# An attention, expert layer and MLP kernel: a new start, new numbers for the order of attention, weight subtracts on one engine, a second bank for transposes of x, and a shifted second tile in the last chunk

## The chip, the cores and the metric

The kernel runs on one core of one Trainium2 chip. The time is the device time of one execution in microseconds (us): 1006.02 us before the change, the median of three runs from 1003.82 to 1007.94 us. The engines are called PE (TensorE: matmuls and transposes; its weight loads are listed apart as PEld), DVE (VectorE), ACT (ScalarE), POOL (GpSimd) and SP (SyncE, which only issues transfers here). Each has its own list of instructions and works through it in order.

## What is computed

```python
def _attn_ref(q, k, v, tau):            # q, k, v: 4 x 8 heads x 576 x 64, float32
    scores = scale * np.matmul(q, k.transpose(0, 1, 3, 2))
    thresh = np.max(scores, axis=-1, keepdims=True) - tau
    scores = np.where(scores >= thresh, scores, -1000000000.0)
    ...                                 # softmax over what is left
    return np.matmul(attn, v)

def _moe_ref(x, w_gate, w_output_gate, w1, w2):     # 2304 tokens, 512 wide, 8 experts of 1024
    e_idx = np.argmax(x @ w_gate, axis=1)           # each token goes to one expert
    ...
        h = np.maximum(x[mask] @ w1[e], 0.0)
        out[mask] = gate_w[mask, None] * eom[mask, e, None] * (h @ w2[e])

def _moe2_ref(x, w_in, w_out):                      # 2304 tokens, 512 -> 2048 -> 512
    h = x @ w_in
    return np.maximum(0.01 * h, h) @ w_out
```

The three run one after the other on the same tokens.

## The kernel before

Every fp32 factor of a product is split into two parts that PE multiplies at full rate: `hi`, a rounded copy, and `lo`, the difference between the number and its `hi` part. A product of two such factors takes three matmuls (hi by hi, hi by lo, lo by hi). So each operand costs a copy (`hi`) and a subtract (`lo`) on the engines beside PE.

The order on every engine is set ahead of time by a list planner, `Plan.run`. Each piece of work is added with the engine or engines it may run on, a cost for each, a priority (`prio`), an earliest time (`at`), the pieces it depends on, and the ring slots it takes and gives back (`Ring(n)`: n buffers or PSUM banks in turn). The planner takes, on the engine that can start soonest, the piece with the lowest priority number, and where two engines are named it takes the one that ends sooner. Its times are its own; on the chip only the order of each engine is left, and the waits on data.

There are four parts.

**Attention, 16 pairs of heads.** For a pair, k, q and v are loaded (`load`, `load_v`, tiles rk, rq, rv, by SP), split into tiles srk and srq (L310 to L317: `hi` is a CAST, `lo` a TENSOR_TENSOR; on POOL, but on ACT and DVE for pair 0), transposed on PE (L341, L367), copied out of PSUM (L250 on ACT, L252 on DVE, and L256 or L258 with the scale for q), multiplied to scores (L465), reduced to the row maximum (L474 DVE), passed through exp (L485 ACT), masked (L493 DVE), transposed (L522), and multiplied with v (L601). tile sw holds k's parts the other way round. The numbers `st.w_...` at the end of the kernel are terms of the priorities of these pieces. In the first microseconds DVE also fills some constant tiles for the router (`consts`, L770 to L787).

**The router and the seam.** The scores of the gates are made beside the last pairs, tokens are counted per expert, and the fullest expert's first 216 tokens are begun before a branch (`tc.If`) on the counts.

**The experts, in windows of 400 to 216 tokens.** SP loads weights into four `raw` tiles of 128 x 1024 in turn; `hi` (L1554, ACT or DVE) and `lo` (L1559, DVE or POOL) put them into the tile named arena. POOL gathers the tokens of a window into tiles sm (L1627). PE transposes each gathered tile of up to 108 tokens into one PSUM bank (`xt`, L1636, ring `r_tp`), from where an L1554 copy and an L1559 subtract take the parts of x out. The first layer is L1667, its relu L1675 (ACT) and L1681 (DVE), the second layer L1708. Beside this the weights of the MLP are packed into integers by L1304, L1310, L1316, L1322 (ACT) and L1326, in tiles dw and cv.

**The second MLP, chunks of 512 tokens and a last one of 256.** For each of 16 slices f of the hidden layer: the first product (L1870, `h2`), 0.01 h on ACT (L1877, `t`), the maximum on DVE (L1881, `g`), `hi` and `lo` of g (L1554, L1559), and the second product (L1896, `out`), for all token tiles of the chunk, the first product running eight slices ahead. At a chunk's end each token tile of 128 is scaled out of PSUM (L1919, `oev`) and stored to its rows by POOL (L1925, `st`). The last chunk has two token tiles, and both are finished by the last slice's six matmuls.

Of the kernel before, what the change touches and what calls it, by code (L numbers as in the profile page):

```python
# [206 lines left out]
def attention(ctx, tc, q, k, v, st):  # L207
# [61 lines left out]
    pl.add("dve", 2.0, lambda o: st.consts(o), [cnt], 10, label="consts", at=8.0)  # L269

    for P in range(NP):
# [6 lines left out]
        def load(o, P=P, b=b, h0=h0, src=None, nm=None):  # L278
            t = raw_p.tile([128, 9, D], F32, tag=nm, name=nm)
            nc.sync.dma_start(  # L280
# [3 lines left out]
            for h in range(2):  # L284
                nc.sync.dma_start(out=t[64 * h:64 * h + 64, 8, :], in_=src[b, h0 + h, 512:576, :])
# [40 lines left out]
        for nm in ("rk", "rq"):  # L326
# [1202 lines left out]
def experts(pl, ctx, tc, st, R, ar, w1, w2, w_in, w_out, xrows, yT, wtab, wf, out):  # L1529
# [8 lines left out]
    r_l1, r_tp, r_l2 = Ring(3), Ring(1), Ring(1)  # L1538
# [7 lines left out]
    def ev(n, ptr=0.0):  # L1546
        return (0.16 + 0.00083 * n + ptr, 0.14 + 0.00106 * n + ptr)
# [26 lines left out]
    for r, n, tw in wins:  # L1574
# [7 lines left out]
        for q in range(4 if r is None else 0, 8):  # L1582
# [13 lines left out]
            if r is None and q < 6:  # L1596
# [14 lines left out]
                *((("dve", "pool"), (1.5, 2.7)) if r is not None else ("dve", 1.4)), lambda o, f=lo, ld=ld, h=a: f(o, ld, h), [a], need - 11.9, rel=[(r_raw, ld)], label="lo", at=free + 3 if r is None else free)  # L1611
# [214 lines left out]
    r_o, r_g, r_t, r_h2 = Ring(1), Ring(2), Ring(2), Ring(4)  # L1826
# [5 lines left out]
    for ci, (c0, n) in enumerate(chunks):  # L1832
# [25 lines left out]
        outs = None  # L1858
        for f in range(FF // 128):
# [23 lines left out]
            def g_hi(o, tt, n=n):  # L1883
                copy(o, ar.g(o.slots[r_g][0])[:, 0, 0:n], tgs[tt.slots[r_t][0]][:, 1, 0:n])

            def g_lo(o, tt, gh, n=n):
                t = ar.g(gh.slots[r_g][0])
                subtract(o, t[:, 1, 0:n], tgs[tt.slots[r_t][0]][:, 1, 0:n], t[:, 0, 0:n].bitcast(F32))

            def prod(o, first, gh, f=f, u=u, c2=c2, m=m):  # L1890
# [15 lines left out]
            gh = pl.add(AD, (0.62, 0.4), lambda o, tt=tt, f=g_hi: f(o, tt), [gg], bf + 3.2, acq=[(r_g, 1)], label="gh")  # L1906
            gl = pl.add("dve", 0.74, lambda o, tt=tt, gh=gh, f=g_lo: f(o, tt, gh), [gh], bf + 3.3, rel=[(r_t, tt)], label="gl")
# [156 lines left out]
```

## Time and profile before

| | us |
|---|---|
| median of three runs | 1006.02 (1003.82 to 1007.94) |
| the profiled execution | 1004.9 |
| its span | 1002.7 |
| PE busy | 960.8 (96%) |
| DVE busy | 641.3 (64%) |
| ACT busy | 507.3 (51%) |
| POOL busy | 264.4 (26%) |

The profile is one execution, taken by the hardware profiler. Times in it count from the start of its span. A row of the timeline has the start and the length of a group of equal instructions on one engine, the source line, what is written and read with the shapes, the count, and in brackets the idle time ahead of it and what ended that. Line numbers are those of the kernel before. In the changed kernel the lines of attention stand one further down; of the later ones L1554 is L1555, L1559 is L1560, L1627 is L1628, L1636 is L1637, L1667 is L1668, L1708 is L1709, L1870 is L1873, L1896 is L1905.

### The profile page before, as it was taken

What the parts mean: (1) busy time and instruction counts of PE and PEld (TensorE: products, weight loads), DVE (VectorE), ACT (ScalarE), POOL (GpSimd) and SP (SyncE); (2) the same over time, 40 slices, a digit from 0 to 9 for tenths busy, and PEclk for the clock granted to TensorE, in tenths of its full rate; (3) what the DMA queues carried; (4) which work ended last, traced back from release to release, by engine and by line L of the source; (5) the groups of instructions that cost most, each with busy time, mean ns of one, the idle gap of its engine ahead of it and who ended that gap; (6) DMA issues with size and microseconds to landing.
All of it is one profiled execution on the core that took longest, in us unless ns stands there. A gap on an engine that the chain in (4) does not pass through costs nothing. (4 is left out here: it accounts for less than half of the span.)

```text
span 1002.7 us, 16909 instructions
## 1 busy us (share of the span) xinstructions
PE 960.8 (96%) x6118; PEld 844.5 (84%) x6118; DVE 641.3 (64%) x1231; ACT 507.3 (51%) x1009; POOL 264.4 (26%) x325
## 2 busy tenths in 40 slices
PE   6999999999999889999899999999999999999994
PEld 6788888888887789989899998888888888888883
DVE  7888998998996775988986548983223223222331
ACT  7778787888874355454555435443223222322321
POOL 4433333333112444442446402321000100100000
PEclk9999999999999899999999999999999999999998
DMA  5523432431242688589887552422000200100000
GB/s 143 150 71 90 129 72 74 138 81 49 75 152 69 191 222 293 190 303 305 301 286 266 166 178 77 119 70 74 11 1 1 84 1 0 63 1 1 18 25 22
DMA packets 63578, 114.32 MB, mean 114 GB/s; under 512 B 15424, under 2 KB 32832, under 8 KB 62976
## 3 DMA queue, kind: packets, MB, share of 16 engines
q1 hardware_dynamic: 56912, 92.02, 29.4%
q0 software_dynamic: 6576, 21.15, 7.6%
q8 instruction: 50, 0.82, 0.3%
q14 instruction: 40, 0.33, 0.1%
HBM read 84.72 MB, written 19.09 MB: 104 GB/s over the span
## 5 line engine op out<-in xcount | busy, mean ns | idle before, releaser
L1870 PE MATMUL ps<-arena 128*128 128x512 f32 (+1 forms) x960 | 207.6, 368 | 0.0
L1896 PE MATMUL ps<-arena 128*128 128x512 f32 x864 | 206.8, 389 | 0.0
L1870 PEld LDWEIGHTS ps<-arena 128*128 128x128 f32 x960 | 168.7, 188 | 30.9
L1559 DVE TENSOR_TENSOR arena<-raw,arena 128x512 fp32r<-128x512 f32 (+2 forms) x131 | 122.7, 941 | 111.1 <-PE ps L1896 67.0
L1896 PEld LDWEIGHTS ps<-arena 128*128 128x128 f32 x864 | 161.3, 188 | 33.2 <-ACT arena L1554 0.2
L1554 ACT CAST arena<-raw 128x1024 fp32r<-128x1024 f32 (+2 forms) x153 | 121.4, 803 | 107.5 <-PE ps L1896 56.4
L1881 DVE TENSOR_TENSOR raw<-ps,raw 128x512 f32<-128x512 f32 (+1 forms) x80 | 50.6, 636 | 134.3 <-ACT raw L1877 134.2
L1708 PE MATMUL ps<-arena 128*128 128x216 f32 (+7 forms) x864 | 128.9, 307 | 6.4 <-ACT arena L1675 4.7
L1708 PEld LDWEIGHTS ps<-arena 128*128 128x128 f32 x864 | 122.7, 193 | 7.4 <-ACT arena L1675 5.1
L1667 PE MATMUL ps<-arena 128*128 128x400 f32 (+7 forms) x768 | 114.1, 308 | 8.7 <-ACT arena L1554 3.2
L493 DVE SCALAR_TENSOR_TENSOR em<-ps,th,e 128x576 f32<-128x576 f32 x144 | 115.6, 811 | 9.2 <-ACT e L485 8.4
L1877 ACT ACTIVATE raw<-ps 128x512 f32<-128x512 f32 (+1 forms) x80 | 43.9, 553 | 150.9 <-PE ps L1870 150.9
L1667 PEld LDWEIGHTS ps<-arena 128*128 128x128 f32 x768 | 110.9, 190 | 10.3 <-DVE arena L1559 3.7
L474 DVE TENSOR_REDUCE nm<-ps 128x1 f32<-128x576 f32 x144 | 107.3, 752 | 17.0 <-PE ps L465 15.2
L485 ACT ACTIVATE e<-ps,nm 128x576 f32<-128x576 f32 x144 | 105.9, 744 | 6.8 <-DVE nm L474 6.2
L465 PE MATMUL ps<-k,qt 128*128 128x288 f32 x512 | 99.5, 322 | 2.3 <-ACT qt L256 0.9
L1925 POOL DMA_INDIRECT out_dram<-sm,oidx x18 | 17.8, 987 | 302.7 <-ACT sm L1919 269.8
L250 ACT COPY eta<-ps 128x512 f32<-128x512 f32 (+1 forms) x152 | 79.4, 543 | 23.3 <-PE ps L522 19.9
L522 PE MATMUL ps<-ident,em 128*128 128x128 f32 x576 | 84.2, 274 | 2.1 <-DVE em L493 1.3
L465 PEld LDWEIGHTS ps<-k,qt 128*128 128x128 f32 x512 | 74.6, 193 | 8.2 <-DVE em L493 2.5
L1559 POOL TENSOR_TENSOR arena<-raw,arena 128x1024 fp32r<-128x1024 f32 x23 | 58.8, 2562 | 61.7 <-ACT arena L1554 59.9
L601 PE MATMUL ps<-eta,rv 128*64 128x288 f32 x512 | 69.5, 412 | 1.9 <-ACT eta L250 1.9
(221 smaller groups left out, 1087.7 us busy)
## 6 DMA issues: line engine op xcount, KB each, us to landing
raw<-in_moe_w_dram SPq DMA_DIRECT2D x70, 512.0 KB
k<-k POOLq DMA_DIRECT2D x30, 304.0 KB
dw<-in_moe_w_in_dram SPq DMA_DIRECT2D x16, 512.0 KB
dw<-in_moe_w_out_dram SPq DMA_DIRECT2D x16, 512.0 KB
rk<-in_k_dram SPq DMA_DIRECT2D x16, 256.0 KB
rq<-in_q_dram SPq DMA_DIRECT2D x16, 256.0 KB
rv<-in_v_dram SPq DMA_DIRECT2D x16, 256.0 KB
xrows<-xt SPq DMA_DIRECT2D x4, 1024.0 KB
```

The source lines that it names most:

```text
L250: nc.scalar.copy(out=out, in_=in_)
L465: nc.tensor.matmul(out=s[:, c, :], lhsT=lhs, rhs=T[kk, P][:, off + c * HALF:off + (c + 1) * HALF], start=(m == 0), stop=(m == 2 * len(ops) ...
L474: nc.vector.tensor_reduce(out=T["nm", n], in_=T["sc", n], axis=AX.XY, op=ALU.max, negate=True)
L485: nc.scalar.activation(out=T["e", n].rearrange("p (a c) -> p a c", a=2), in_=T["sc", n], func=AF.Exp, bias=T["nm", n][:, 0:1], scale=1.0,)
L493: nc.vector.scalar_tensor_tensor(out=T["em", P, t][:, h, :].rearrange("p (a c) -> p a c", a=2), in0=T["sc", n], scalar=T["th", n][:, 0:1], ...
L522: nc.tensor.transpose(out=bank(o)[:, c * 128:(c + 1) * 128], in_=T["em", P, t][:, h, 64 * h + c * 128:64 * h + (c + 1) * 128], identity=ident,
L1554: nc.scalar.copy(out=out, in_=in_)
L1559: (nc.vector if o.eng == "dve" else nc.gpsimd).tensor_tensor(out=out, in0=in0, in1=in1, op=ALU.subtract)
L1667: nc.tensor.matmul(out=bank(o)[:, 0:n], lhsT=w[:, wi, 128 * f:128 * f + 128], rhs=xx[:, xi, c, :], start=(c == 0 and i == 0), stop=(c == K ...
L1708: nc.tensor.matmul(out=bank(first, d)[:, 0:n], lhsT=w[:, wi, k0:k0 + 128], rhs=hx[:, xi, :], start=(f == 0 and i == 0), stop=(f == 7 and i ...
L1870: nc.tensor.matmul(out=bank(o)[:, 0:n], lhsT=w[:, wi, c, 128 * c2:128 * c2 + 128], rhs=y[:, c, 0:n], start=(k == 0), stop=(k == 3 * KD - 1),)
L1896: nc.tensor.matmul(out=bank(first, t), lhsT=g[:, gi, 128 * t:128 * t + 128], rhs=w[:, wi, c2, :], start=(f == 0 and k == 0), stop=(f == FF ...
```

## The change

Five things are changed together.

- Pair 0's q is loaded on ACT's queue and no longer behind k on SP's; q's `lo` of pair 0 goes to POOL; the constants of the router may come at 1.9 and no longer at 8.0 in the planner's time.
- The numbers `st.w_...` that set the order of attention are new.
- `lo` of the experts' weights is on DVE alone, at a planned cost of 1.25 and no longer 1.5 (or 2.7 on POOL).
- The ring `r_tp` for the transposed x has two PSUM banks and no longer one.
- In the last chunk g takes half a slot (ring `r_gs`, four halves), the second product is a piece for each token tile, and the priority of the second tile's pieces lies three slices (`BEHIND`) later. The `oev` of a tile depends on that tile's last product.

```diff
-    pl.add("dve", 2.0, lambda o: st.consts(o), [cnt], 10, label="consts", at=8.0)
+    pl.add("dve", 2.0, lambda o: st.consts(o), [cnt], 10, label="consts", at=1.9)
...
-            nc.sync.dma_start(
+            eng = nc.scalar if (nm, P) == ("rq", 0) else nc.sync
+            eng.dma_start(
...
-                "sp", 1.75, lambda o, f=load, src=src, nm=nm: f(o, src=src, nm=nm),
-                [], base - 27, after=[O.get(("rk", P))],
+                "act" if (nm, P) == ("rq", 0) else "sp", 1.75, lambda o, f=load, src=src, nm=nm: f(o, src=src, nm=nm),
+                [], base - 27, after=[O.get(("rk", P)) if P else None],
...
-                *(("dve", 0.65) if P == 0 else ("pool", 1.36)), lambda o, f=lo, nm=nm: f(o, nm=nm), [a], base - 13.9,
+                *(("dve", 0.65) if P == 0 and nm == "rk" else ("pool", 1.36)), lambda o, f=lo, nm=nm: f(o, nm=nm), [a], base - 13.9,
...
-    r_l1, r_tp, r_l2 = Ring(3), Ring(1), Ring(1)
+    r_l1, r_tp, r_l2 = Ring(3), Ring(2), Ring(1)
...
-                *((("dve", "pool"), (1.5, 2.7)) if r is not None else ("dve", 1.4)), lambda o, f=lo, ld=ld, h=a: f(o, ld, h), [a], need - 11.9, rel=[(r_raw, ld)], label="lo", at=free + 3 if r is None else free)
+                "dve", 1.25 if r is not None else 1.4, lambda o, f=lo, ld=ld, h=a: f(o, ld, h), [a], need - 11.9, rel=[(r_raw, ld)], label="lo", at=free + 3 if r is None else free)
...
+            def g_at(o, n=n):
+                if n > 256:
+                    return ar.g(o.slots[r_g][0])[:, :, 0:n]
+                i = o.slots[r_gs][0]
+                return ar.g(i // 2)[:, :, 256 * (i % 2):256 * (i % 2) + n]
...
+            if small:
+                for t in range(2):
+                    o = pl.add(
+                        "pe", 3 * 0.228, lambda o, gh=gh, f=prod, fb=outs, t=t: f(o, fb or o, gh, ts=(t,)), [gl, *wo, tiles[t], outs],
+                        bf + 5.4 + 5.4 * BEHIND * t, acq=[(bk, 2), (r_o, 1)] if outs is None else [], rel=[(r_gs, gh)] if t else [], label="out")
+                    outs = outs or o
+                    tiles[t] = last_o = o
+                continue
...
-    st.w_k = [-17.57, -56.75, -17.26, -9.64, -5.15]
+    st.w_k = [-12.16, -50.35, -23.14, -10.04, -5.04]
...
```

On DVE the program begins, after some fills of tiles, with pair 0's k and q. Before the change these rows stand there (srk and srq are the split k and q, sw is k's parts swapped, qsc and ntau are made from tau):

```order
L312 CAST srk<-rk 128x9x64
L317 TENSOR_TENSOR srk<-rk,srk 128x9x64
L324 CAST sw<-srk 128x9x64
L252 CAST k_233<-ps 128x512
L317 TENSOR_TENSOR srq<-rq,srq 128x9x64
L1984 TENSOR_SCALAR qsc<-tt 128x1
L1985 TENSOR_SCALAR ntau<-tt 128x1
L770 MEMSET ones 128x128
```

After the change the same place on DVE, from the last of the constants on, reads:

```order
L785 TENSOR_SCALAR scr<-tid 128x20
L786 CAST tt<-scr 128x20
L788 MEMSET capr 128x1 x8
L313 CAST srk<-rk 128x9x64
L313 CAST srq<-rq 128x9x64
L318 TENSOR_TENSOR srk<-rk,srk 128x9x64
L2003 TENSOR_SCALAR qsc<-tt 128x1
L2004 TENSOR_SCALAR ntau<-tt 128x1
L325 CAST sw<-srk 128x9x64
L252 CAST k_273<-ps 128x512
```

All thirteen rows of constants (L771 to L788) have moved ahead of k's copy, the copy of q (before on ACT) has moved between k's copy and k's subtract, and q's subtract has gone to POOL.

On PE the first windows of the experts follow the seam. Before, the transposes of x (L1636, ident is the unit matrix, sm the gathered tokens) and the layers stand in this order, up to the first layer of the window of 400 tokens:

```order
L1708 MATMUL ps<-arena 128x216 x12
L1636 MATMUL ps<-ident,sm_70 128x108 x4
L1708 MATMUL ps<-arena 128x216 x36
L1636 MATMUL ps<-ident,sm_71 128x108 x4
L1708 MATMUL ps<-arena 128x216 x36
L1636 MATMUL ps<-ident,sm_72 128x108 x4
L1708 MATMUL ps<-arena 128x216 x12
L1636 MATMUL ps<-ident,sm_73 128x76 x4
L1667 MATMUL ps<-arena 128x400 x96
```

After the change the same place on PE reads:

```order
L1709 MATMUL ps<-arena 128x216 x12
L1637 MATMUL ps<-ident,sm_70 128x108 x4
L1709 MATMUL ps<-arena 128x216 x12
L1637 MATMUL ps<-ident,sm_71 128x108 x4
L1709 MATMUL ps<-arena 128x216 x24
L1637 MATMUL ps<-ident,sm_72 128x108 x4
L1637 MATMUL ps<-ident,sm_73 128x76 x4
L1709 MATMUL ps<-arena 128x216 x48
L1637 MATMUL ps<-ident,sm_70 128x108 x4
L1637 MATMUL ps<-ident,sm_71 128x108 x4
L1668 MATMUL ps<-arena 128x400 x96
```

The last transposes of this window's x (76 tokens of sm_73) have moved from directly ahead of its first layer to 48 matmuls ahead of it, and the first two tiles of the window after it stand there now.

On PE the program ends with the last chunk of the MLP, first products (128x256) between second products (128x512). Before:

```order
L1870 MATMUL ps<-arena 128x256 x12
L1896 MATMUL ps<-arena 128x512 x6
L1870 MATMUL ps<-arena 128x256 x12
L1896 MATMUL ps<-arena 128x512 x18
L2059 UNCONDITIONAL_BRANCH
```

After:

```order
L1873 MATMUL ps<-arena 128x256 x12
L1905 MATMUL ps<-arena 128x512 x6
L1873 MATMUL ps<-arena 128x256 x12
L1905 MATMUL ps<-arena 128x512 x27
L2078 UNCONDITIONAL_BRANCH
```

Nine more second products stand behind the last first product. By the banks they write, the last nine are the second token tile's alone (its last three slices of three matmuls), so the first tile's last product stands ahead of nine others and no longer in the last six.

On POOL the gathers of x after the seam stand one behind the other, and no weight subtracts of 128 x 1024 but one are left there; 22 have gone to DVE (23 to 1 on POOL, 51 to 73 on DVE).

## Rows read from the trace of the kernel before

**Rows 1.** Busy time by stretch: PE, PEld, DVE, ACT, POOL; clock, DMA share, GB/s.

```profile
20.00:320.00 300.00, 294.40 (x2371) 247.65 (x2369) 261.31 (x628) 235.67 (x530) 102.47 (x200) 1.00 0.36 96
400.00:525.00 125.00, 119.88 (x834) 118.42 (x833) 112.41 (x156) 62.51 (x105) 50.84 (x29) 1.00 0.82 277
605.00:985.00 380.00, 380.00 (x1767) 318.25 (x1766) 156.39 (x236) 120.12 (x215) 36.96 (x31) 1.00 0.11 35
```

**Rows 2.** What PE waited for, 339 to 606 us: total, times, longest.

```profile
PE ps L1708 <- ACT arena L1675: 4.7, 1, 4.7
PE ps L1667 <- ACT arena L1554: 3.2, 2, 1.7
PE ps L1667 <- DVE arena L1559: 2.9, 3, 1.3
PE ps L1667 <- DVE arena L1681: 2.6, 2, 1.8
```

**Rows 3.** Timeline and one stretch of the first microseconds.

```profile
2.50:3.00 0.50, 0.00 (x0) 0.00 (x0) 0.00 (x0) 0.00 (x0) 0.32 (x2) 1.00 0.99 344
...
4.05 0.75 DVE L312 CAST srk<-rk 128x576 fp32r<-128x576 f32 x1 [1.58 <-DMA rk<-in_k_dram]
...
4.84 0.76 DVE L317 TENSOR_TENSOR srk<-rk,srk 128x576 fp32r<-128x576 f32 x1
...
5.65 1.25 PE L341 MATMUL ps<-identr,srk 128*128 128x128 f32 x8 [5.65 <-DVE srk L317]
6.08 0.67 ACT L310 CAST srq<-rq 128x576 fp32r<-128x576 f32 x1 [0.57 <-DMA rq<-in_q_dram]
...
7.89 0.17 DVE L770 MEMSET ones<- 128x128 bf16 x1
...
9.48 0.16 DVE L787 MEMSET capr<- 128x1 f32 x8
...
10.22 3.01 PE L465 MATMUL ps<-k,qt 128*128 128x288 f32 x11 [0.91 <-ACT qt L256]
...
12.33 1.41 POOL L317 TENSOR_TENSOR srk<-rk,srk 128x576 fp32r<-128x576 f32 x1
```

**Rows 4.** Groups of one shape, 400 to 525 us: count, busy us, mean ns.

```profile
L1559 POOL TENSOR_TENSOR arena<-raw,arena 128x1024 fp32r<-128x1024 f32 x13 | 33.7, 2599 | 18.8 <-ACT arena L1554 18.7
...
L1304 DVE TENSOR_SCALAR cv<-dw 128x512 int32<-128x512 int32 x18 | 22.5, 1252 | 4.5 <-DMA dw<-in_moe_w_out_dram 4.2 <-DMA dw<-in_moe_w_in_dram 0.3
L1326 DVE SCALAR_TENSOR_TENSOR cv<-dw,cv 128x512 f32<-128x512 f32 x18 | 19.7, 1095 | 2.6 <-ACT dw L1322 1.9
L1559 DVE TENSOR_TENSOR arena<-raw,arena 128x1024 fp32r<-128x1024 f32 x16 | 19.1, 1216 | 0.3 <-ACT arena L1554 0.2
```

**Rows 5.** Timeline: L1304 and L1326 on DVE with POOL busy, and without.

```profile
416.67 5.46 DVE L1304 TENSOR_SCALAR cv<-dw 128x512 int32<-128x512 int32 x1
...
417.08 4.75 POOL L1559 TENSOR_TENSOR arena<-raw,arena 128x1024 fp32r<-128x1024 f32 x2
...
430.96 0.69 DVE L1326 SCALAR_TENSOR_TENSOR cv<-dw,cv 128x512 f32<-128x512 f32 x1
...
433.41 0.42 DVE L1304 TENSOR_SCALAR cv<-dw 128x512 int32<-128x512 int32 x1
```

**Rows 6.** Timeline: the start of the window of 400 tokens.

```profile
355.74 0.42 ACT L1554 CAST arena<-ps 128x304 fp32r<-128x304 f32 x1
...
356.21 0.45 PE L1667 MATMUL ps<-arena 128*128 128x400 f32 x1 [1.44 <-ACT arena L1554]
```

**Rows 7.** Timeline: the end of the program.

```profile
984.62 4.27 PE L1896 MATMUL ps<-arena 128*128 128x512 f32 x18
...
988.70 1.26 ACT L1919 ACTIVATE sm<-ps,mt 128x512 f32<-128x512 f32 x2 [2.48 <-PE ps L1896]
989.66 0.98 POOL L1925 DMA_INDIRECT out_dram<-sm,oidx  x1 [31.12 <-ACT sm L1919]
993.16 0.98 POOL L1925 DMA_INDIRECT out_dram<-sm,oidx  x1 [2.51 <-DMA out_dram<-sm,oidx]
```

More of the change, by code (lines that the diff above doesn't have):

```diff
@@ L284, in load @@
             for h in range(2):
-                nc.sync.dma_start(out=t[64 * h:64 * h + 64, 8, :], in_=src[b, h0 + h, 512:576, :])
+                eng.dma_start(out=t[64 * h:64 * h + 64, 8, :], in_=src[b, h0 + h, 512:576, :])
             T[nm, P] = t
@@ L1825, in experts @@
     chunks = [(c, min(512, NT - c)) for c in range(0, NT, 512)]
-    r_o, r_g, r_t, r_h2 = Ring(1), Ring(2), Ring(2), Ring(4)
+    r_o, r_g, r_t, r_h2, r_gs = Ring(1), Ring(2), Ring(2), Ring(4), Ring(4)
+    BEHIND = 3
     tgs = [ys_ for ys_ in st.tg]
@@ L1857, in experts @@
         AHEAD = 8
-        outs = None
+        outs, before, tiles = None, last_o, [None] * m
         for f in range(FF // 128):
@@ L1881, in act_g, with g_hi, g_lo, prod @@
                 nc.vector.tensor_tensor(out=t[:, 1, 0:n], in0=bank(a)[:, 0:n], in1=t[:, 0, 0:n], op=ALU.max)
[L1883 to L1890, printed above, removed]
+            def g_at(o, n=n):
[3 more added lines that the diff above has]
+                return ar.g(i // 2)[:, :, 256 * (i % 2):256 * (i % 2) + n]
+            def g_hi(o, tt, n=n, at=g_at):
+                copy(o, at(o)[:, 0], tgs[tt.slots[r_t][0]][:, 1, 0:n])
+            def g_lo(o, tt, gh, n=n, at=g_at):
+                t = at(gh)
+                subtract(o, t[:, 1], tgs[tt.slots[r_t][0]][:, 1, 0:n], t[:, 0].bitcast(F32))
+            def prod(o, first, gh, f=f, u=u, c2=c2, ts=range(m), at=g_at):
                 w = V[u, 1].rearrange("p a (c f) -> p a c f", c=2)
-                g = ar.g(gh.slots[r_g][0])
+                g = at(gh)
                 k = 0
                 for gi, wi in ((0, 0), (0, 1), (1, 0)):
-                    for t in range(m):
+                    for t in ts:
                         nc.tensor.matmul(
@@ L1905, in experts @@
             gg = pl.add("dve", ev(n)[1], lambda o, a=a, tt=tt, f=act_g: f(o, a, tt), [tt], bf + 3.1, rel=[(bk, a), (r_h2, a)], label="g")
-            gh = pl.add(AD, (0.62, 0.4), lambda o, tt=tt, f=g_hi: f(o, tt), [gg], bf + 3.2, acq=[(r_g, 1)], label="gh")
-            gl = pl.add("dve", 0.74, lambda o, tt=tt, gh=gh, f=g_lo: f(o, tt, gh), [gh], bf + 3.3, rel=[(r_t, tt)], label="gl")
+            small = m == 2
+            gh = pl.add(AD, (0.36, 0.3) if small else (0.62, 0.4), lambda o, tt=tt, f=g_hi: f(o, tt), [gg, before if small else None], bf + 3.2,
+                        acq=[(r_gs if small else r_g, 1)], label="gh")
+            gl = pl.add("dve", 0.45 if small else 0.74, lambda o, tt=tt, gh=gh, f=g_lo: f(o, tt, gh), [gh], bf + 3.3, rel=[(r_t, tt)], label="gl")
+            if small:
[6 more added lines that the diff above has]
+                continue
             last_o = pl.add(
@@ L1928, in st_o @@
                 )
[L1930 removed]
+            e = pl.add(AD, ev(512, 0.1), lambda o, fb=outs, f=oev: f(o, fb), [tiles[t] or last_o, e, mts[c0 // 128 + t]], base + CH + t, acq=[(r_sm, 1)],
                        rel=[(bk, outs), (r_o, outs)] if t == m - 1 else [], label="oev")
@@ L1946, in tile_attn_moe_mlp @@
     st.nsc, st.ntp, st.nav = 4, 4, 2
-    st.w_k = [-17.57, -56.75, -17.26, -9.64, -5.15]
-    st.w_s, st.w_m, st.w_th, st.w_x, st.w_kk, st.w_t, st.w_te = -0.43, -9.06, -19.95, 1.0, -7.23, 2.59, -17.09
-    st.w_l = [-1.89, 4.35]
-    st.w_av, st.d_av = 17.36, -0.31
-    st.w_xo = 18.47
-    st.w_rt, st.w_ch = 24.07, -0.65
+    st.w_k = [-12.16, -50.35, -23.14, -10.04, -5.04]
+    st.w_s, st.w_m, st.w_th, st.w_x, st.w_kk, st.w_t, st.w_te = -0.89, -35.52, -19.15, -8.2, -33.71, 2.67, -15.54
+    st.w_l = [3.23, -18.37]
+    st.w_av, st.d_av = 15.0, -0.31
+    st.w_xo = 17.9
+    st.w_rt, st.w_ch = 33.28, -8.79
     st.w_n0, st.w_n1 = 60, 60
```

1 line of the change is left out of this document (removed).

## The prediction

> **What bounds the kernel now.** I read the page first: PE is busy 96% of the span, so a gain must come from a stretch where PE stands still, or from the ends. Then busy time by stretch [rows 1]: in attention PE is busy 294.4 of 300 us, in the second MLP 380.0 of 380. Both are PE's own pace, and nothing beside PE can shorten them by more than the idle rest. In the experts, from 400 to 525 us, PE lacks 5.1 of 125 us, and DVE is busy 112.4 of them, a share of 0.90. Third, the waits of PE between 339 and 606 us [rows 2]: one of 4.7 us behind the branch of the seam, two of 3.2 us in all for a copy on ACT, three of 2.9 us for a subtract on DVE, two of 2.6 us for a relu on DVE. The last three lines, 8.7 us in seven waits, are what the change can reach in the experts; the 4.7 us come out of the branch, which is not touched. Last the two ends of the timeline [rows 3, 7]: at the start PE's first scores come at 10.22 us, and at the end two stores follow each other 3.50 us apart.
>
> **The change part by part. The tail.** PE's last 18 matmuls start at 984.62 and release the scaling at 988.70 [rows 7]: 4.08 / 18 = 0.227 us each. The first token tile's last product now stands ahead of nine more, so its scaling may come 9 x 0.227 = 2.04 us earlier, at 986.66, and its store at 987.62 instead of 989.66. The second tile is ready when it was, PE's work being the same. Today its store waits for the first one's data to land (released by the DMA [rows 7]), 993.16 - 989.66 = 3.50 us after it; with the first store at 987.62 that gives 991.12, which is still later than its own data at 989.66. So both stores move by 2.04 us, and the end with them. Bounds: 0, if what follows the stores sets the end by itself, and 3.5, if the spacing went as well. I take -2.0, since the chain runs through the two stores in the trace.
>
> **The second bank and the place of the transposes.** Before the window of 400 tokens the first matmul waits 1.44 us for the copy of the last tile of x, which ends at 355.74 + 0.42 = 356.16 [rows 6]; PE starts 0.05 us later. With two banks the order puts 48 matmuls of 216 columns between that transpose and the layer. By the pace above, 0.227 us for 512 columns, they last 48 x 0.227 x 216 / 512 = 4.6 us, three times the wait, and cover it. The same distance covers the subtract of x behind the copy, which ends most of the three waits for DVE. So 3.2 and 2.9 us go. What is late next is the relu: 2.6 us of waits stand behind DVE's other work. Half of it, 1.3 us, should go with the stretched rows below. Bounds of this part: -3.2 (the copies alone) and -8.7 (all).
>
> **The subtracts on DVE alone.** 22 of 128 x 1024 move from POOL to DVE; 22 x 1.216 = 26.8 us in all, 13 x 1.216 = 15.8 us of it between 400 and 525 us [rows 4]. In the same stretch DVE's other rows are longer than they need be. L1304 takes 5.46 us while POOL subtracts for 4.75 us, and 0.42 us where POOL is free [rows 5]; its 18 take 22.5 us together, against 18 x 0.42 = 7.6, and the 18 of L1326 take 19.7 against 18 x 0.69 = 12.4 [rows 4, 5]. So 14.9 + 7.3 = 22.2 us come back when POOL no longer subtracts. DVE goes to 112.4 + 15.8 - 22.2 = 106.0 of 125 us: emptier, not fuller. But the 22 now stand in DVE's line ahead of relus and of the parts of x. Today DVE ends five waits of 5.5 us with 51 subtracts of its own; 22 more would by proportion bring 5.5 x 22 / 51 = 2.4 us of new ones. Bounds 0 and 3.7 (all seven waits in proportion, 8.7 x 22 / 51). I take +2.4. The experts then come to -3.2 - 2.9 - 1.3 + 2.4 = -5.0 us, between -8.7 and -0.8 (only the copies go, new waits as taken). The gathers on POOL, no longer behind subtracts, are done earlier; nothing waits for them in rows 2, so this is worth nothing here.
>
> **The start.** DVE idles 1.58 us until 4.05 us, when k has landed [rows 3], so it is free from 2.47. The constants take 7.89 to 9.64, 1.75 us, and now stand there: until 4.22, 0.17 us past k. Then comes q's copy, which is ahead of k's subtract in DVE's order, for another 0.75 us. So k's subtract begins at 4.22 + 0.75 + 0.75 = 5.72 instead of 4.84, 0.9 us later, and PE's first row (released by it at 5.65) with it. Behind that PE works on without a break to the scores, which move too: +0.9. Moving q to ACT's queue gives little in return: q's copy came at 6.08 and now comes at 4.97 at the earliest, but PE stands ahead of it, and q's subtract on POOL takes 1.41 us [rows 3] where DVE takes 0.76. Bounds: -1.1, if the scores follow q's copy alone, and +1.8, if k lands later as well. For that landing a row has the price: the DMA engines are busy to 0.99 in 2.50 to 3.00 us and move 344 GB/s, so 128 x 576 x 4 bytes of q in among k's would hold k back by 0.86 us; in the next microsecond it is latency and not the engines, so I take none of it.
>
> The Trainium skill, "DMA: Bandwidth & Descriptors", section "Issuing engines are not separate DMA queues", says that transfers issued by different engines share the same 16 DMA engines and interleave, and that a second issuer saves only issuing time. That speaks against the early q. By that rule the start would be the +1.8 above, and the sum 0.9 us worse; the busy share of 0.99 agrees with it, for that half microsecond alone.
>
> **The order of attention.** Row by row only the first three pairs and the last two of 16 differ. PE lacks 5.6 us in 300 [rows 1]; five pairs of sixteen hold 5.6 x 5 / 16 = 1.75 of them, so -1.7 to +1.7, and I take 0: no row gives a sign, and at the seam the branch's wait stays.
>
> **The sum:** -2.0 - 5.0 + 0.9 + 0 = -6.1 us. On the profiled execution of 1004.9 (span 1002.7, 2.2 around it) this gives 998.8. That execution lies 1.1 us below the median of 1006.02, inside the runs' spread of 4.1; against the median the sum is 999.9. I take the middle, 999.3.
>
> **The rivals.** First, slower than before: DVE becomes the bound of the experts. If the long rows are not given back (because they are long for another reason than POOL), DVE needs 112.4 + 15.8 = 128.2 us of work in 125: 3.2 us more than there is if it never idles, 142.4, or 17.4 more, at its share of 0.90. Halfway this is some +10, and with the tail, the copies and the start 1004.9 + 10 - 2.0 - 3.2 + 0.9 = 1010.6. It decides once less than 15.8 of the 22.2 us come back. Against it stands the pair of rows 5, where nothing but POOL's rows differs. Second, the waits only change place: the experts gain 0.8, and 1004.9 - 2.0 - 0.8 + 0.9 = 1003.0. For it speaks that three engines feed each window. Third, the start and the new order of attention cost their upper bounds, 1.8 and 1.7: 1004.9 - 2.0 - 5.0 + 3.5 = 1001.4. Fourth, all 8.7 us of waits go, no new one comes, and the start follows q: 1004.9 - 2.0 - 8.7 - 1.1 = 993.1. That the change does not do what it says is a part of the second: the orders do show every move, so what can fail is the effect.
>
> **How the numbers follow.** The forecast has 0.52 (own range 996 to 1001.5), all waits gone 0.16, waits only moved 0.16, a dear start and order 0.10, DVE as the bound 0.06. A measurement of this kernel can tell about 0.5%, 5.0 us, from no change. The forecast of -6.1 is beyond that in most of its range, some four fifths of its chance, 0.42, and with a part of the dear start, 0.04, and all waits gone, 0.16, faster has 0.62; slower is the DVE rival and a little of the moved waits, 0.07; the rest, 0.31, is within. The range from 993 to 1004 takes in the two middle rivals and most of the high gain and leaves out the DVE case.
>
> **What would show it.** Right: PE's waits for L1554 and L1559 at the start of first layers are gone, L1304 and L1326 have means near 0.42 and 0.69 us, DVE is near 106 us between 400 and 525, the first store is 2.0 us earlier against PE's last matmul, PE's first row at about 6.6 us and the first scores at about 11.1. Wrong: relus (L1681) as the end of more waits than 3.7 us, DVE over 115 us in that stretch, the stores less than 3.5 us or no longer tied to each other, or an attention that ends over 2 us away from today's.

## The result, and the profile after

The changed kernel takes 993.71 us, the median of seven runs (992.16 to 996.98), against 1006.02 of the kernel before (1001.35 to 1009.75, seven runs): a ratio of 0.9893, 95% interval 0.9873 to 0.9914. The profiled execution took 992.9 us, its span 991.0, where before it was 1004.9 and 1002.7. So it gained 12 us where 6.1 were forecast: inside the range, at the time of the fourth rival, and about twice the likeliest sum.

Where the 11.7 us of span went can be read off four points of PE's timeline. The first scores come at 11.87 us (before 10.22), the first second layer of the experts at 338.12 (339.05), the first product of the MLP at 585.61 (595.38), and the second store of the last chunk at 981.50 (993.16). The start lost 1.65, and up to the experts all of it came back and 0.9 more. The experts' stretch, from PE's first L1709 to its first L1873, fell from 256.3 to 247.5, a gain of 8.8. From there to the last store it is 395.9 instead of 397.8, a gain of 1.9. Together 0.9 + 8.8 + 1.9 = 11.6; the spans differ by 11.7.

The experts' stretch as a whole, before and after, the columns as in [rows 1] (the second number is PE's busy time, the one behind the counts the granted clock, as a share of PE's 2.4 GHz):

```profile
339.05:595.38 256.33, 246.03 (x1752) 242.73 (x1753) 193.25 (x266) 126.37 (x218) 112.15 (x68) 0.98 0.77 250
338.12:585.61 247.49, 243.64 (x1752) 242.17 (x1753) 181.64 (x289) 129.65 (x219) 54.65 (x46) 0.98 0.79 261
```

PE stands still for 10.3 us of it before and for 3.9 after, 6.4 less, and its busy time is 2.4 less at the same mean clock.

Busy time by stretch in the changed kernel, the columns as in [rows 1]; the experts' part of it stands 12 us earlier here:

```profile
20.00:320.00 300.00, 295.75 (x2380) 248.63 (x2379) 261.59 (x625) 238.81 (x541) 101.70 (x198) 1.00 0.36 95
388.00:513.00 125.00, 125.00 (x860) 124.25 (x859) 103.48 (x173) 66.66 (x110) 19.91 (x17) 1.00 0.86 296
593.00:973.00 380.00, 380.00 (x1768) 318.37 (x1767) 157.43 (x236) 120.84 (x216) 38.22 (x31) 1.00 0.11 35
```

In the middle row PE is busy all of its 125 us, where before it lacked 5.1, and DVE is busy 103.5 us, where before it was 112.4, although it does more. What PE waited for between 300 and 606 us, as in [rows 2]:

```profile
PE ps L1709 <- ACT arena L1676: 3.8, 1, 3.8
PE ps L1637 <- DMA sm<-xrows,gidx: 3.7, 1, 3.7
```

Three others of 0.2 to 0.3 us each are left out. All seven waits of 8.7 us are gone; the branch's wait is still there, and one large new one has come, for a gather of x. The groups of DVE in the same 125 us, to be laid beside [rows 4]:

```profile
L1560 DVE TENSOR_TENSOR arena<-raw,arena 128x1024 fp32r<-128x1024 f32 x33 | 40.0, 1217 | 8.0 <-ACT arena L1555 7.8
...
L1311 DVE SCALAR_TENSOR_TENSOR cv<-dw,cv 128x512 int32<-128x512 int32 x18 | 12.2, 684 | 0.2
L1327 DVE SCALAR_TENSOR_TENSOR cv<-dw,cv 128x512 f32<-128x512 f32 x16 | 10.9, 684 | 0.3
L1305 DVE TENSOR_SCALAR cv<-dw 128x512 int32<-128x512 int32 x18 | 7.5, 419 | 4.4 <-DMA dw<-in_moe_w_in_dram 3.0 <-DMA dw<-in_moe_w_out_dram 1.4
```

L1305 has a mean of 419 ns (before 1252), L1327 of 684 (before 1095). A third line, which [rows 4] does not show, came back as well. Before, it read:

```profile
L1310 DVE SCALAR_TENSOR_TENSOR cv<-dw,cv 128x512 int32<-128x512 int32 x18 | 16.6, 920 | 0.4
```

The subtract itself is as long as it was, 1217 ns, and there are 33 instead of 16.

The start, in the timeline, against [rows 3]:

```profile
5.60 0.75 DVE L313 CAST srk<-rk 128x576 fp32r<-128x576 f32 x1 [1.32 <-DMA rk<-in_k_dram]
...
6.27 0.74 DVE L313 CAST srq<-rq 128x576 fp32r<-128x576 f32 x1
...
6.93 0.75 DVE L318 TENSOR_TENSOR srk<-rk,srk 128x576 fp32r<-128x576 f32 x1
7.10 1.86 POOL L318 TENSOR_TENSOR srq<-rq,srq 128x576 fp32r<-128x576 f32 x1 [4.20 <-DMA vt<-in_v_dram]
...
7.72 1.58 DVE L325 CAST sw<-srk 128x576 fp32r<-128x576 f32 x1
7.73 1.26 PE L342 MATMUL ps<-identr,srk 128*128 128x128 f32 x8 [7.73 <-DVE srk L318]
...
11.87 1.89 PE L466 MATMUL ps<-k,qt 128*128 128x288 f32 x8
```

DVE was free and waited for k's data until 5.60, not until 4.05 as before. And the last rows, against [rows 7]:

```profile
977.03 0.69 ACT L1938 ACTIVATE sm<-ps,mt 128x512 f32<-128x512 f32 x1 [1.86 <-PE ps L1905]
978.00 0.98 POOL L1944 DMA_INDIRECT out_dram<-sm,oidx  x1 [29.16 <-ACT sm L1938]
979.07 0.69 ACT L1938 ACTIVATE sm<-ps,mt 128x512 f32<-128x512 f32 x1 [1.35 <-PE ps L1905]
981.50 0.98 POOL L1944 DMA_INDIRECT out_dram<-sm,oidx  x1 [2.52 <-DMA out_dram<-sm,oidx]
```

The two scalings are now 979.07 - 977.03 = 2.04 us apart, and the stores still 3.50.

### The profile page after: what moved, and what is told of

It reads as the page before. It is cut to its first block, busy times and chain, and to the rows that moved or that the text cites. A ratio compares the mean times of both kernels' runs of the same rounds, so it can differ in the third digit from the quotient of the medians.

```text
span 991.0 us, 16885 instructions
## 1 busy us (share of the span) xinstructions
PE 957.1 (97%) x6118; PEld 843.0 (85%) x6118; DVE 630.8 (64%) x1251; ACT 509.9 (51%) x1011; POOL 208.8 (21%) x303
## 5 line engine op out<-in xcount | busy, mean ns | idle before, releaser
L1560 DVE TENSOR_TENSOR arena<-raw,arena 128x1024 fp32r<-128x1024 f32 (+2 forms) x153 | 142.3, 936 | 108.7 <-PE ps L1905 58.4
L1873 PE MATMUL ps<-arena 128*128 128x512 f32 (+1 forms) x960 | 207.8, 368 | 0.0
L1873 PEld LDWEIGHTS ps<-arena 128*128 128x128 f32 x960 | 168.8, 188 | 30.9
L1709 PE MATMUL ps<-arena 128*128 128x216 f32 (+7 forms) x864 | 127.5, 306 | 3.9 <-ACT arena L1676 3.8
L1709 PEld LDWEIGHTS ps<-arena 128*128 128x128 f32 x864 | 122.3, 193 | 4.7 <-ACT arena L1676 4.2
L1668 PE MATMUL ps<-arena 128*128 128x400 f32 (+7 forms) x768 | 112.6, 307 | 0.0
L1668 PEld LDWEIGHTS ps<-arena 128*128 128x128 f32 x768 | 110.6, 190 | 0.0
L1944 POOL DMA_INDIRECT out_dram<-sm,oidx x18 | 18.4, 1024 | 301.2 <-ACT sm L1938 268.2
L523 PEld LDWEIGHTS ps<-ident,em 128*128 128x128 f32 x576 | 67.7, 141 | 3.4 <-DVE em L494 1.8
```

The costliest lines, as they stand in the source:

```text
L523: nc.tensor.transpose(out=bank(o)[:, c * 128:(c + 1) * 128], in_=T["em", P, t][:, h, 64 * h + c * 128:64 * h + (c + 1) * 128], identity=ident,
L1560: (nc.vector if o.eng == "dve" else nc.gpsimd).tensor_tensor(out=out, in0=in0, in1=in1, op=ALU.subtract)
L1668: nc.tensor.matmul(out=bank(o)[:, 0:n], lhsT=w[:, wi, 128 * f:128 * f + 128], rhs=xx[:, xi, c, :], start=(c == 0 and i == 0), stop=(c == K ...
L1709: nc.tensor.matmul(out=bank(first, d)[:, 0:n], lhsT=w[:, wi, k0:k0 + 128], rhs=hx[:, xi, :], start=(f == 0 and i == 0), stop=(f == 7 and i ...
L1873: nc.tensor.matmul(out=bank(o)[:, 0:n], lhsT=w[:, wi, c, 128 * c2:128 * c2 + 128], rhs=y[:, c, 0:n], start=(k == 0), stop=(k == 3 * KD - 1),)
```

## The experiments

The runs came from three chips, on which the kernel before took 1004.5, 1013.0 and 1005.2 us (medians). So ratios to the kernel before on the same chip are compared, and lengths of stretches; "the stretch" is the experts' one, from PE's first second-layer product to the first product of the MLP.

**Which of the two edits in the experts made the gain.** Two of the five parts act there: the subtracts and the bank. They were tried in all four combinations. First the subtracts given back to POOL:

```diff
-                "dve", 1.25 if r is not None else 1.4, lambda o, f=lo, ...
+                *((("dve", "pool"), (1.5, 2.7)) if r is not None else ("dve", 1.4)), lambda o, f=lo, ...
```

> The changed kernel with one part undone: the lo subtracts of the experts' weights may go to POOL again (21 of 128 x 1024 do), two banks kept. Measure: the experts' stretch, from PE's first L1709 to its first L1873; 256.3 us in the kernel before, 247.5 in the changed one. Theory A (POOL's subtracts hold DVE up, and that is what ended most waits): most of the 8.8 us are lost again, stretch 253 to 256 us, L1305 on DVE back to a mean over 1 us, waits for DVE at L1668 back; time about 1000. Theory B (the single bank was the cause; DVE's long rows lay in idle time): stretch at most 1.5 us longer, 249, time about 995.

Measured: 1002.7 us, ratio 0.997 (0.9948 to 0.9992), stretch 257.0. PE's waits and, from the timeline, the longest of them with what DVE and POOL did before:

```profile
PE ps L1668 <- DVE arena L1682: 5.7, 4, 4.1
...
PE ps L1637 <- DMA sm<-xrows,gidx: 4.0, 1, 4.0
```

```profile
480.74 4.95 POOL L1560 TENSOR_TENSOR arena<-raw,arena 128x1024 fp32r<-128x1024 f32 x2 [2.31 <-ACT arena L1555]
...
481.63 1.81 DVE L1305 TENSOR_SCALAR cv<-dw 128x512 int32<-128x512 int32 x1
483.48 2.77 DVE L1311 SCALAR_TENSOR_TENSOR cv<-dw,cv 128x512 int32<-128x512 int32 x1
...
488.70 2.53 POOL L1560 TENSOR_TENSOR arena<-raw,arena 128x1024 fp32r<-128x1024 f32 x1 [1.56 <-ACT arena L1555]
488.91 2.62 DVE L1305 TENSOR_SCALAR cv<-dw 128x512 int32<-128x512 int32 x1
...
498.85 0.46 DVE L1682 SCALAR_TENSOR_TENSOR arena<-ps,arena 128x296 fp32r<-128x296 f32 x1
...
499.37 1.85 PE L1668 MATMUL ps<-arena 128*128 128x296 f32 x6 [4.06 <-DVE arena L1682]
```

This shows the path by which a held-up row reaches PE. Three rows of DVE start while POOL subtracts and take 1.81, 2.77 and 2.62 us in place of 0.42, 0.69 and 0.42: 5.7 us late in sum. The relu L1682 stands behind them in DVE's line, which has hardly a gap from there on, and ends at 499.31; PE waits 4.06 us for it. The wait costs more than itself, since PE's granted clock falls to the lower of its two levels (0.50, 1.2 GHz) with it:

```profile
498.00:505.00 7.00, 5.63 (x23) 5.63 (x24) 5.32 (x12) 3.40 (x8) 0.00 (x0) 0.52 0.97 349
```

In the 10 us before and after that row it was 1.00. Over the stretch PE stands still for 9.8 us (changed 3.9) and is busy for 247.2 (changed 243.6). Theory A holds, also in size (256 was the upper end, 257.0 came).

The other undoing: one bank, with the subtracts on DVE.

```diff
-    r_l1, r_tp, r_l2 = Ring(3), Ring(2), Ring(1)
+    r_l1, r_tp, r_l2 = Ring(3), Ring(1), Ring(1)
```

> The changed kernel with one part undone: one PSUM bank for the transposed x, subtracts on DVE alone kept. Same measure (before 256.3, changed 247.5 us). Theory A (POOL): 1 to 3 us longer at most, and the new wait of 3.7 us for a gather ahead of the window of 400 is gone, since its second transpose is no longer pulled ahead: stretch 246 to 249 us. Theory B (bank): the waits of 3.2 us for ACT's copy and 2.9 us for the subtract of x come back, stretch 252 to 254 us, time about 999.

Measured: 992.88 us, ratio 0.9882 (0.9847 to 0.9917), stretch 246.2, a little shorter than with two banks. The waits:

```profile
PE ps L1668 <- DVE arena L1560: 2.0, 1, 2.0
PE ps L1668 <- ACT arena L1555: 0.7, 1, 0.7
```

Of the seven waits of [rows 2] only the pair at the window of 400 comes back, 2.7 us; in its place the 3.7 us for the gather are gone. The waits at the later windows, which the prediction had given to the bank, do not come back with one bank.

Then each alone on the kernel before. The subtracts alone:

> The kernel before with one part of the change: lo of the weights on DVE alone. Same measure, from PE's first L1708 to its first L1870 (256.3 us before). Theory A (POOL): L1304 falls from a mean of 1.25 to about 0.42 us, the waits for DVE go and the stretch falls by 6 to 9 us to 247 to 250. Theory B (bank): the waits of L1667 for the copy of x stay, and the 22 subtracts bring some 2.4 us of new waits: 255 to 257. If parts add up, this one and the bank alone make 8.8 us together.

Measured: 995.71 us, ratio 0.9906 (0.987 to 0.9943), stretch 247.5. Its waits are those of one bank:

```profile
PE ps L1667 <- DVE arena L1559: 2.0, 1, 2.0
PE ps L1667 <- ACT arena L1554: 0.7, 1, 0.7
PE ps L1667 <- DVE arena L1681: 0.2, 1, 0.2
```

The bank alone:

> The kernel before with one part of the change: two PSUM banks for the transposed x. Same measure (256.3 us before). Theory A (POOL): 253 to 256, since DVE is held up as before and ends other waits. Theory B (bank): 6.1 us less, 250, with no wait of a first L1667 for L1554 or L1559; the price may be a wait for a gather, as the 3.7 us in the changed kernel.

Measured: 1004.58 us, ratio 1.0005 (0.9986 to 1.0024), stretch 257.1.

```profile
PE ps L1667 <- DVE arena L1681: 6.2, 4, 4.1
...
PE ps L1636 <- DMA sm<-xrows,gidx: 3.7, 1, 3.7
```

So of 256.3 us before, the subtracts alone make 247.5, the bank alone 257.1, both 247.5. The whole gain of the experts is the subtracts'. The bank did end the waits for ACT's copy and for x's subtract, as forecast, but 6.2 us for the relu stand in their place while POOL subtracts, and 3.7 us for a gather in any case.

**What of POOL's subtract is to blame.** Its way is longer (2.6 us against 1.2), and its presence holds DVE up. To have the second without the first, DVE did all subtracts, and POOL did some again, in place into a tile that was no longer needed:

```diff
                 subtract(o, t[:, 1, :], raw[ld.slots[r_raw][0]], t[:, 0, :].bitcast(F32))
+                if r is not None and (8 * r + q) % 3 == 0:
+                    s = raw[ld.slots[r_raw][0]]
+                    nc.gpsimd.tensor_tensor(out=s, in0=s, in1=t[:, 0, :].bitcast(F32), op=ALU.subtract)
```

> The changed kernel, and POOL does again, beside it, 21 or 22 of the 64 weight subtracts, in place into the raw tile after DVE has read it; no product depends on what POOL makes. Output unchanged. It tells POOL's presence from POOL's slowness: before, a subtract on POOL took 2.6 us and the product waited for it, and it may also have held DVE up. Theory A1 (POOL's reads hold DVE up): L1305 goes back from 0.42 to a mean over 0.8 us, PE's waits for DVE come back, stretch over 252 us (changed 247.5), time about 1000. Theory A2 (the longer way from the raw tile to the product through POOL was the cause): L1305 stays near 0.42 us, stretch 247 to 249. The raw tiles come free some 3 us later in both, as they did before the change.

The edit read `r` and `q` after the loop had ended, so POOL did 66 subtracts again and not 22. Measured at that dose: 1095.37 us, ratio 1.0821 (1.079 to 1.0853), stretch 348.8. DVE's own subtracts and PE's largest wait:

```profile
L1560 DVE TENSOR_TENSOR arena<-raw,arena 128x1024 fp32r<-128x1024 f32 x73 | 144.8, 2000 | 33.4 <-ACT arena L1555 33.4
...
PE ps L1671 <- DVE arena L1685: 49.2, 8, 12.9
```

The same with the indices bound, 22 subtracts done again:

> As d1, with 22 of the 64 weight subtracts done again on POOL (d1 had come out with all 66 of a longer list, since the edit read its indices late). No product depends on what POOL makes. Theory A1 (POOL's reads hold DVE up; d1 showed it at three times the dose): L1305 on DVE at a mean of 0.7 us or more in place of 0.42, PE's waits for DVE back, stretch 251 to 258 us (changed 247.5). Theory A2 (what cost in the kernel before was the longer way of a weight through POOL, and d1 was hurt by the later freeing of every raw tile): L1305 near 0.42, stretch 247 to 249.

Measured: 1028.99 us, ratio 1.0247 (1.0218 to 1.0276), stretch 282.6.

```profile
L1560 DVE TENSOR_TENSOR arena<-raw,arena 128x1024 fp32r<-128x1024 f32 x73 | 102.1, 1411 | 29.7 <-ACT arena L1555 29.1 <-PE ps L1671 0.6
...
L1327 DVE SCALAR_TENSOR_TENSOR cv<-dw,cv 128x512 f32<-128x512 f32 x20 | 18.0, 901 | 0.3
...
L1305 DVE TENSOR_SCALAR cv<-dw 128x512 int32<-128x512 int32 x20 | 9.7, 491 | 9.6 <-DMA dw<-in_moe_w_in_dram 7.1 <-DMA dw<-in_moe_w_out_dram 2.4
```

```profile
PE ps L1671 <- DVE arena L1685: 15.3, 6, 5.0
PE ps L1640 <- DMA sm<-xrows,gidx: 8.1, 1, 8.1
```

With 0, 22 and 66 useless subtracts on POOL, DVE's subtract of 128 x 1024 takes 1217, 1411 and 2000 ns, and PE waits 0, 15.3 and 49.2 us for the relu (L1682, here L1685). That POOL's presence alone holds DVE up and that this reaches PE is shown. But the expectation's own sign, L1305 over 0.7 us, failed (0.49): the hold-up fell on other rows, since POOL's second subtract can only start when DVE's has ended. And the stretch grew by 35 us, not by 4 to 10. Its row, to be laid beside that of the changed kernel in the section on the result:

```profile
338.31:620.93 282.62, 255.39 (x1752) 252.23 (x1753) 206.68 (x289) 127.06 (x218) 118.89 (x68) 0.93 0.71 228
```

PE stands still for 27.2 us of it (changed 3.9), and its own rows take 255.4 us (changed 243.6) at a granted clock of 0.93 and not 0.98. So of the 35 us some 23 are waits and some 12 are PE's slower pace beside them. Among the waits the raw tiles' later freeing and the gather queued behind the extra subtracts (8.1 us, changed 3.7) were not separated from DVE's hold-up.

**The new wait for a gather.** In the changed kernel two transposes of the next window's x stand directly ahead of the window of 400, and the second one waits for its rows. An order that lets them stand only behind that window's first products:

```diff
-            b = pl.add("pe", 0.45, lambda o, f=xt, g=g: f(o, g), [g], lead, acq=...
+            b = pl.add("pe", 0.45, lambda o, f=xt, g=g: f(o, g), [g], lead, after=[O.get(("L1first", wi_ - 1)) if r else None], acq=...
...
+                O.setdefault(("L1first", wi_), pe)
```

> The changed kernel, but a window's transposes of x may stand only behind the first matmuls of the window before it; in the changed kernel two of them stand ahead of the window of 400 and one waits 3.7 us for its gather. Theory (that wait is a new one, made by the second bank with the order that the planner makes of it): the wait goes, the stretch from PE's first L1709 to its first L1873 falls from 247.5 to 243.7 to 245, time about 990. Rival (PE would wait there for the weights of the window of 400 anyway, by DMA or subtract): 246 to 247.5, with a wait for L1560 or L1555 in place of the gather, as with one bank (2.7 us).

Measured: 993.27 us, ratio 0.9803 (0.9774 to 0.9832), stretch 244.8, as expected; no wait for a gather, and no wait of a first L1668 for L1560 in its place. The rival falls. The expectation compared chips: on this one, two runs with the wait for the gather (the old tail and the old order, below) have stretches of 252.2 and 252.6, so here the mend goes with 7.4 to 7.8 us and not 2.7. The size of the ratio owes something to the chip as well: the kernel before ran at a granted clock of 0.983 to 0.988 there, this one at 0.991 to 0.992.

**The tail.** The last chunk as before, all else changed (`small = False`, full slots of g, `oev` behind the last product of both tiles):

```diff
-            small = m == 2
+            small = False
```

> The changed kernel with the last chunk as before: both token tiles in each slice's six products, g in whole slots. Measure: from PE's first L1873 to the end of the span, 407.3 us in the kernel before, 405.4 in the changed one. If the shifted second tile alone made this: 407.3, and the two stores again 3.5 us apart, the first 0.9 to 1.0 us after the last product's scaling; time 2 us above the changed kernel's. If the 1.9 us came from elsewhere (the weights' new subtracts, the state of the clock): 405.4.

Measured: 1000.83 us, ratio 0.9891 (0.9858 to 0.9924) on the chip where the kernel with the gather fixed had 0.9803. Its stores:

```profile
985.66 0.98 POOL L1944 DMA_INDIRECT out_dram<-sm,oidx  x1 [30.84 <-ACT sm L1938]
989.17 0.98 POOL L1944 DMA_INDIRECT out_dram<-sm,oidx  x1 [2.52 <-DMA out_dram<-sm,oidx]
```

From the MLP's first product, at 591.49 us here, to the second store it is 397.7 us; before 993.16 - 595.38 = 397.8, changed 981.50 - 585.61 = 395.9. To the end of the span it is 998.7 - 591.5 = 407.2, where 407.3 was expected. The same length is 405.4 us in all ten traces with the shifted tile and 407.2 to 407.3 in the four without it. The 1.9 us are the shifted tile's.

**The start and the order of attention.** The old numbers for the order, with the new start:

```diff
-    st.w_k = [-12.16, -50.35, -23.14, -10.04, -5.04]
+    st.w_k = [-17.57, -56.75, -17.26, -9.64, -5.15]
...
```

> The changed kernel with the old numbers for the order of attention; start, subtracts, banks and tail as changed. Measure: PE's first scores (10.2 us in the kernel before, 11.9 in the changed one) and its last gate product, L660 (321.5 before, 320.8 changed). Theory A (the start costs 1.6 us to the end of attention, the new order earns 2.3): last L660 at 323 us, time some 2 us above the changed kernel's. Theory B (a late start is made up within the first pairs whatever the order, and the order earns the 0.7 alone): 321.5, time within 1 us of the changed kernel's.

Measured: 1002.71 us, ratio 0.989 (0.9853 to 0.9927). The last L660 comes at 326.6 us, later than both theories had it. On the same chip, with the new numbers and the same start, it came at 321.8 (the run with the old tail) and 323.1 (the gather fixed). One row shows a part of it, in PE's timeline, a wait for the transfer k<-k, which is 1.1 us in the run with the old tail:

```profile
28.89 0.63 PE L466 MATMUL ps<-k,qt 128*128 128x288 f32 x3 [2.61 <-DMA k<-k]
```

So with the new start the new numbers are worth 3.5 to 4.8 us. Then both as before, all else changed:

> The changed kernel with the start and the numbers for the order of attention both as before; subtracts, banks and tail as changed. Measure: PE's last gate product, L660, 320.8 us in the changed kernel, 321.5 in the kernel before, and 326.6 with the old numbers and the new start. Theory A (the two belong together and are worth nothing as a pair): 320.5 to 321.8, time within 1.5 us of the changed kernel's. Theory B (the pair is worth some us, hidden by what varies from run to run): 323 or more, time 2 us or more above the changed kernel's.

Measured: 994.74 us, ratio 0.9904 (0.9877 to 0.9931), last L660 at 321.8. The yardstick on that chip:

> The changed kernel itself, unedited, as the yardstick on this chip for the three others. All theories: ratio to the kernel before 0.987 to 0.991, stretch from PE's first L1709 to its first L1873 247 to 249 us, one wait of 3.5 to 4 us for a gather, tail as before.

Measured: 994.35 us, ratio 0.9902 (0.9873 to 0.9931), stretch 248.7, wait for the gather 4.1 us, last L660 at 322.3. Theory A: start and order as a pair are worth nothing that can be measured. The ratios differ by 0.0002, with intervals of 0.003 to either side, and the last L660 by 0.5 us, while executions of one order differ there by up to 1.6 us (320.2 to 321.8 on one chip, in the two runs with the new start and order).

Last, the start mended in the new order, together with the mended gather: q's load back on SP's queue and q's copy on POOL, and nothing moved in between.

```diff
-            eng = nc.scalar if (nm, P) == ("rq", 0) else nc.sync
+            eng = nc.sync
...
-                (nc.vector if o.eng == "dve" else nc.gpsimd).tensor_copy(out=t[:, :, 0, :], in_=T[nm, P])
+                (nc.vector if o.eng == "dve" and nm == "rk" else nc.gpsimd).tensor_copy(out=t[:, :, 0, :], in_=T[nm, P])
```

> The kernel with transposes held behind the first matmuls of the window before, and pair 0's q loaded on SP's queue behind k again and its copy made on POOL, in the place of DVE. The order of everything else is that of the changed kernel. Theory A (k landed 1.5 us late, at 5.6 in place of 4.05, because q's load on a second queue took its share of the DMA engines, and q's copy cost k's subtract 0.7): k's copy starts by 4.3 us, PE's first row at 5.8 to 6.0, first scores at 10.3 to 10.9 in place of 11.9. Theory B (k lands late for another reason): copy of k at 5.5. For the end of attention (last L660): if the first pairs are paced by DVE, little of a 1 us gain is left there. Time 4 to 5 us below the changed kernel's: 3.7 of the gather's wait and the rest of the start.

Measured: 988.09 us (987.69 to 990.21), ratio 0.9838 (0.981 to 0.9865), where the changed kernel had 994.35 on the same chip: 6.3 us less. (By the ratio to the kernel before on its chip the run with the gather alone mended, 0.9803, is as good; the intervals overlap.) Its start:

```profile
4.21 0.75 DVE L313 CAST srk<-rk 128x576 fp32r<-128x576 f32 x1
4.99 0.76 DVE L318 TENSOR_TENSOR srk<-rk,srk 128x576 fp32r<-128x576 f32 x1
...
5.81 1.25 PE L342 MATMUL ps<-identr,srk 128*128 128x128 f32 x8 [5.81 <-DVE srk L318]
...
11.03 2.18 PE L466 MATMUL ps<-k,qt 128*128 128x288 f32 x8
```

With q behind k on one queue, k's copy starts at 4.21, right behind the constants, and with no wait for data; PE's first row comes at 5.81. Theory A holds for k, with one thing left open: v's load, which had moved forward to 3.12 us when q left SP's queue, went back to 4.91 with this edit, and its share is not told apart from q's. The first scores, at 11.03, are 0.1 us behind the expectation's end: PE waits 1.55 us in between for DVE's copy into sw, which starts at 7.39, since the row ahead of it waits 1.51 us for tau (loaded behind q on the same queue now), and takes 1.07 us beside POOL's subtract of q. At the last L660 it is 321.5 against 322.3. The stretch is 241.6 against 248.7, 7.1 us less, of which 4.1 are the gather's wait. Most of the rest is PE's clock behind that wait. From 359.60 to 365.40 us, first in the changed kernel on this chip, then in this run:

```profile
359.60:365.40 5.80, 5.78 (x19) 5.75 (x20) 3.07 (x6) 0.97 (x3) 1.00 (x1) 0.50 0.96 338
359.60:365.40 5.80, 5.80 (x33) 5.80 (x33) 5.08 (x10) 4.68 (x10) 0.00 (x0) 1.00 1.05 377
```

Right behind the wait, which ends at 359.62, the clock stood at its lower level, 0.50, and 19 products of PE fall into the row; in the mended order there is no wait, the clock stayed at 1.00, and 33 do. Over the stretch PE's busy time is 3.0 us shorter (241.5 against 244.4).

## Why the prediction was right, and where its terms were off

**The sign, the range and the tail.** The sum was -6.1 us and -12.0 came on the profiled executions. The tail was right in mechanism and size: forecast -2.0, shown -1.9, with 2.04 us between the scalings and 3.50 between the stores, both as forecast.

**The subtracts on DVE alone.** The refund was right in the two rows that were priced: L1305 was to fall to 0.42 and came to 0.419, L1327 to 0.69 and came to 0.684. The third line, L1311, was left out of it and gave back another 4.4 us. DVE between 400 and 525 us was to fall to 106.0 of 125 and fell to 103.5; that this is so near is in part luck, since the same stretch took up 17 more subtracts and not 13. The first rival, DVE as the bound, needed less than 15.8 of the 22.2 us back and is out. A rule of the Trainium skill, "SBUF — State Buffer", section "Who interferes with whom", fits what the rows show: it says that a two-port instruction of DVE, or one with two inputs in SBUF, and one of GpSimd that reads SBUF shut each other out, and that the first to start holds the shared port until it is done. In the run with the subtracts given back, POOL's 2.53 us start at 488.70 and DVE's 0.42 us become 2.62 from 488.91.

The step that failed here is the +2.4 us of new waits, taken in proportion to the count of subtracts. There was none: no wait for a subtract or a relu is left in the changed kernel. Counting subtracts was the wrong scale. The waits of before were not ended by DVE's subtracts as such but by rows that POOL had made long, so with those gone a DVE that is busy 0.83 of the time, in rows of about 1.2 us, was early enough for every relu. For the same reason the relu's 2.6 us went whole, and not by half. Together the two terms are 2.4 + 1.3 = 3.7 us.

**The second bank.** Here the forecast had the right number for the wrong edit. 6.1 us of waits for copies and subtracts of x were given to the second bank. They went, but one bank with the subtracts on DVE does as well (stretch 246.2 against 247.5), and the bank alone does nothing (ratio 1.0005). What [rows 2] names as the releaser, ACT's copy and DVE's subtract, is the last link; what made these links late at the later windows were POOL's subtracts. Only the pair at the window of 400, 2.7 us, was the bank's.

**The gathers.** "Nothing waits for them in rows 2, so this is worth nothing here" failed: in the order that two banks allow, PE's transposes come earlier than the gathered rows land, and 3.7 us of new wait arose, which the mended order removes, together with a stretch at the lower clock behind it that the sum had no term for. The order of PE's rows after the change, listed ahead of the prediction, shows these transposes ahead of the window of 400; their price was not worked out.

**What remains of the experts.** Forecast -5.0, shown -8.8. Terms: -8.7 for the seven waits, +3.7 for the gather, and -1.5 for two waits of PE with no releaser (listed as "issue" under L1708 in the kernel before, at 562 to 564 us, left out of the sum). That makes -6.5, and PE's idle time in the stretch fell by as much; the other 2.3 us are in PE's busy time (246.0 before, 243.6 after) and were not pinned to an edit. The waits with no releaser are not the change's: they stand again, 1.4 to 1.9 us of them between 540 and 575 us, in three runs on one chip that hold the change's subtracts.

**The start.** Forecast +0.9 at the first scores, shown +1.65. The order on DVE cost 0.54 us and not 0.9: k's subtract begins 6.93 - 5.60 = 1.33 us behind k's copy, where before it was 0.79, and the constants were done before k came. What failed is the choice to take none of the price for k's landing: k came 5.60 - 4.05 = 1.55 us later, more than the 0.86 us of the bound, and came back to 4.21 with one queue. Here the rule of the Trainium skill that the prediction quotes was right, and the trace's row for 2.50 to 3.00 us was the sign that bore it out. PE's first row comes 7.73 - 5.65 = 2.08 us later and the scores only 1.65, because PE did not work "without a break to the scores" before: the scores' own row in [rows 3] has a wait of 0.91 us for ACT, which the prediction read over and which is gone after. The loss was then repaid by the order of attention, taken at 0 for want of a sign: the pair is worth nothing that can be measured, though with the new start the order alone is worth 3.5 to 4.8 us.

**The rivals.** The second, waits that only change place, is what the bank alone did, at 1004.58 us. The third, a dear start, came true at the first scores and was repaid. The fourth gave the time, 993.1, but only by half of its mechanism: the 8.7 us did go, but there is a new wait and the start did not follow q. That its figure was met is luck in part, since 3.7 us of new wait and 1.65 at the start stand against the unpriced 2.3 us, the 1.5 us of waits with no releaser and what attention made up.

## What to carry to other kernels

Before a shared piece of work is split between DVE and POOL, look for DVE rows of one shape whose lengths differ several times over, and see whether POOL reads at that moment: here 13 subtracts that POOL took off DVE, 15.8 us of work, held DVE up by some 27 us over three of its lines, and giving all 22 back was worth 8.8 us to PE. A wait's last releaser in the profile need not be its cause; undo one edit at a time in both directions, and the edit that the releaser names may prove worth nothing. When a wait of PE goes, look at the granted clock behind it too: the wait of 4.1 us for the gather went with 3.0 us of PE's own time. When buffers are added, the order may pull work ahead of its data, so look for the transfer that it will now wait for.

## What the runs showed of the hardware

A second load on another queue delayed the first by more than its bytes: 128 x 576 floats of q at 344 GB/s are 0.86 us, and k landed 1.55 us later (5.60 against 4.05), while in one queue, q behind k, k's copy starts at 4.21. Over all traces k's copy starts at 5.16 to 5.99 us in the nine with q on ACT's queue and at 4.05 to 4.33 in the five with q behind k; v's load moved with q's in all of them. POOL is slowed as well: its subtract of 128 x 576 takes 1.86 us beside DVE's subtract and 1.40 us in the mended start, and DVE's copy into sw takes 1.58 us beside it where it took 0.49 before. PE at times stops for 0.2 to 0.9 us with no releaser between 550 and 565 us, in some executions of a kernel and not in others; in the run with the old numbers the granted clock was 0.83 from 560 to 570 us, where it was 1.00 in the 10 us before and after. Twice in the rows above a wait of PE of some 4 us went with a granted clock at its lower level, behind the gather (0.50 from 359.60 to 365.40) and behind the held-up relu (0.52 from 498.00 to 505.00).
